# A mixture-of-experts kernel on one core: weight conversions gathered into two of five slots, and tables, gate scalings and transposes at other steps

## The chip, the core and the metric

The kernel runs on one core of a Trainium2 chip. The core has a matrix engine (TensorE, PE in the profile, with its weight loads as PEld), VectorE (DVE), ScalarE (ACT), GpSimd (POOL) and SyncE (SP), which here issues transfers. Each engine works through its own instructions in order; semaphores order them among each other. The metric is the time of one execution in device microseconds, taken as the median of some runs; less is better. Before the change it is 967.4 us (runs from 965.36 to 968.28).

## The reference

Three things in a row: attention over 32 heads with a threshold below the row's maximum, a mixture of 8 experts in which each of 2304 tokens goes to one expert, and a feed-forward block with weights in float64 on the host (`w_in`, `w_out` reach the kernel as pairs of 32-bit words).

```python
def _attn_ref(q, k, v, tau):            # 4 batches, 8 heads, 576 rows, 64 wide
    scores = scale * np.matmul(q, k.transpose(0, 1, 3, 2))
    thresh = np.max(scores, axis=-1, keepdims=True) - tau
    ...
    return np.matmul(attn, v)

def _moe_ref(x, modality_id, w_gate, modality_bias, w1, w2):     # 2304 tokens, 512 wide, 8 experts
    logits = x @ w_gate + modality_bias[modality_id]
    e_idx = np.argmax(logits, axis=1)
    ...
    for e in range(E):
        h = np.maximum(x[mask] @ w1[e], 0.0)                     # 512 -> 1024
        out[mask] = gate_w[mask, None] * (h @ w2[e])             # 1024 -> 512
    return out

def _moe2_ref(x, w_in, w_out):                                   # 512 -> 2048 -> 512
    h = x @ w_in
    g = h * (1.0 / (1.0 + np.exp(-1.702 * h)))
    return g @ w_out
```

## The kernel before

Every product is made of three in a rounded 32-bit format: a matrix is split into an upper half (ScalarE's cast, names that end in h) and a lower half (VectorE's subtraction, names that end in l), and upper x upper, upper x lower and lower x upper are added up in PSUM.

The kernel has three stages on the core's time line. Attention runs until about 316 us. From 316 to some 546 us run five **slots** of one expert each: four with 512 tokens, the last with 264 (`SLOT_ROWS`). From there to the end run the **last blocks**, five blocks of tokens through the feed-forward weights.

The order on every engine is that in which the code issues instructions; no scheduler moves them. The loop over slots s and steps f = 0 to 7 (from line 1364) fixes it. One step does this:

- the first product S1(s, f), 12 matmuls on line 973 with xh, xl (the slot's tokens, transposed) and ah, al (a quarter of the expert's w1 serves two steps); then hh (ScalarE) and hl (VectorE) from its result. The second product S2, 12 matmuls on line 1017 with hh, hl and bh, bl (w2), trails by two steps (`LAG`);
- `split(g, i)` converts a quarter of the weights, ra to ah and al (i = 0) or rb to bh and bl (i = 1): ah, al of quarter g + 1 in even steps, bh, bl of quarter g in odd steps. `load` issues the transfers of ra and rb, 512 KB each, two quarters ahead, on SyncE's queue;
- tokens of the next slot: `gather_slot` on GpSimd's queue at two steps early in the slot (`F0`), four tiles xg of 128 rows; `scale(t)` multiplies a tile by its gate on ScalarE (line 1218), for all tiles at step 2 in slot 0 and at step 3 later; then four items of `xprep`, each four transposes into one PSUM tile (line 945), xh on ScalarE and xl on VectorE, one at each of the steps that `XP0` (slot 0) and `XP` (later) give: steps 3 to 6 in slot 0, 4 to 7 later. In the last slot the same places take `xsplit` for the first last block (lines 960 and 961);
- **conversions** of the feed-forward weights (`conv`, a `Pipe`): each has three parts, one step or more apart: the load of cv_raw (512 KB, SyncE), the upper part (cv_a on ScalarE, then four VectorE operations, lines 1143 to 1146), the lower part (wi_h or wo_h on ScalarE, wi_l or wo_l on VectorE, lines 1151 and 1152). There are 15 in the slots; one begins at every odd step from slot 1 on: four in each of the slots 1 to 3, three in slot 4;
- `att.sides(6)` twice a step: side work in small pieces, in slot 0 and 1 above all the routing tables for the slots after the first two (`Router.assign("B", ...)`): R, OL (line 861 to 868) on VectorE, sums on TensorE (line 874), the lists for the gathers. A `None` in that list ends a turn.

At the end of a slot its result y (512 x 512) is copied out of PSUM at the next slot's step 1, two tiles each on ScalarE and VectorE, and written by four transfers on SyncE's queue, ahead of the third quarter's weights of that slot. The tiles xg, raw weights and cv_raw have 4, 2 and 2 buffers: a transfer waits until its buffer has been read.

Of the kernel before, what the change touches and what calls it, by code (L numbers as in the profile page):

```python
# [13 lines left out]
ACTF = mybir.ActivationFunctionType  # L14
# [6 lines left out]
DM = H * D  # L21
# [13 lines left out]
CA = (0, 1, 2, 2, 2, 2, 2, 2, 2, 2, 2, 2, 2, 2, 2, 2)  # L35
CB = (0, 0, 0, 1, 0, 1, 0, 1, 0, 1, 0, 1, 0, 0, 0, 0)
HO = True
XP = (0, 0, 0, 0, 1, 1, 1, 9)
XP0 = (0, 0, 0, 1, 1, 1, 1, 9)
NBW = 6  # L40
F0 = (0, 1, 0)
NROW = 2
# [485 lines left out]
SLOT_TILES = tuple(-(-r // 128) for r in SLOT_ROWS)  # L528
# [4 lines left out]
class Router:  # L533
# [168 lines left out]
    def assign(self, ph, gate):  # L702
        nc, wk = self.nc, self.wk[ph]
        first = ph == "A"
# [149 lines left out]
        def low(c0, c1):  # L854
            nc.vector.tensor_tensor(
                OL[:, c0:c1], self.iota.unsqueeze(1).broadcast_to([128, c1 - c0, 128]),
                plf[:, 1, c0:c1].unsqueeze(2).broadcast_to([128, c1 - c0, 128]), op=ALU.is_equal,
            )
# [36 lines left out]
        def compact():  # L895
# [15 lines left out]
            yield  # L911
            self.idx["cB"], self.idx["oB"] = icc, ico

        return [
            None, ranks, pages, starts, limits, slots, inside, counted, places, digits, high,
            lambda: (low(0, 5), values(0)), lambda: (low(5, 10), values(1)), lambda: low(10, n), gate,
            *[None] * (1 if first else NBW), lambda: sum_up(0, n), lists,
            *([] if first else [None] * 12 + [gaps, compact, None, bounds]),
        ]
# [118 lines left out]
def moe_kernel(ctx, tc, kq, v, tau, mid, w_gate, mod_bias, w1, w2, w_in, w_out, out):  # L1038
# [171 lines left out]
    def slot(e_idx, g_rows, raw_tile, w_tile, put):  # L1210
# [1 line left out]
        ev = nc.sync.value_load(e_idx, min_val=0, max_val=NE - 1)  # L1212
        W = {}

        def scale(t):

            g = g_rows[t]
            nc.scalar.activation(g[:, 0:DM], g[:, 0:DM], ACTF.Copy, scale=g[:, DM:DM + 1])  # L1218

        def load(g):  # L1220
            ra = raw_tile("ra", "p (k f) -> p k f", dict(k=4))
# [133 lines left out]
    blocks[0]["load"](1)  # L1355
    att.tail(5)
    for t in range(SLOT_TILES[0]):
        blocks[0]["scale"](t)
    for i, f in enumerate(xq):
        f()  # L1360
        att.tail(2)
# [3 lines left out]
    for s in range(NS):  # L1365
        blk = blocks[s]
        for f in range(8):
            ffn.step(blk, f, (lambda: blk["split"](0, 1)) if f == 1 and HO else None, mid3=lambda: att.sides(6))
            f0 = F0[min(s, 2)]
            if s + 1 < NS and f in (f0, f0 + 1):  # L1370
# [6 lines left out]
                gq = gq[2:]  # L1377
                if f == f0 + 1:
                    xq = make_slot(s + 1)
            if s + 1 < NS and f == (3 if s else 2):  # L1380
                for t in range(SLOT_TILES[s + 1]):
                    blocks[s + 1]["scale"](t)
            if s + 1 == NS and f == f0:
                last, xq = make_last(0)
# [14 lines left out]
            if conv is None:  # L1399
                if not att.tail(6):  # L1400
                    open_resident()
                    wi, wo = R["wi"], R["wo"]
                    conv = Pipe(
                        [piece("i", i, wi, i) for i in range(NWI)] + [piece("o", i, wo, i) for i in range(NWO)])
            elif "gB" in router.idx and (f % 2 == 1 or len(conv.live) > 1):
                conv.step(f % 2)
            for _ in range((XP0 if s == 0 else XP)[f]):
                if xq:
                    xq.pop(0)()
            att.sides(6)  # L1410
# [131 lines left out]
```

## Time and profile before

| | us |
|---|---|
| median of three runs | 967.4 |
| lowest, highest | 965.36, 968.28 |
| the profiled execution | 968.82 |
| its span, from the first to the last instruction | 967.1 |
| TensorE busy in the span | 919.8 (95%) |
| VectorE, ScalarE, GpSimd busy | 512.9, 458.0, 225.5 |

Work is reckoned on the profiled execution, which took 1.4 us more than the median. A busy TensorE is not one at its peak, since the ends of its pipelined matmuls are modelled; so its times are read here from start to start of whole groups, and its waits from the idle time ahead of a matmul. The column PEclk gives the share of TensorE's clock that was granted: 1.00 is its 2.4 GHz level and 0.50 its 1.2 GHz level.

### The profile page before, as it was taken

How to read it: one execution, taken by the hardware profiler on the slowest of the kernel's cores; microseconds unless marked ns; L12 is line 12 of the kernel's file. 1: busy time of each engine (PE TensorE's matmuls, PEld its weight loads, DVE VectorE, ACT ScalarE, POOL GpSimd, SP SyncE). 2: the span in 40 equal slices, each digit the busy share in tenths (PEclk: the TensorE clock that was granted, in tenths of full speed). 3: DMA queues.
4: the chain of work that ended last, by engine and by line, in shares of the span. 5: the costliest groups of instructions: out<-in, count | busy, mean ns of one | idle time of the engine just before them, and what ended most of it. 6: DMA issues, size and time to landing. Idle time of an engine off the chain costs nothing.

```text
span 967.1 us, 13933 instructions
## 1 busy us (share of the span) xinstructions
PE 919.8 (95%) x5015; PEld 740.3 (77%) x5015; DVE 512.9 (53%) x1125; ACT 458.0 (47%) x824; POOL 225.5 (23%) x299
## 2 busy tenths in 40 slices
PE   8899999999988989999998899999999999999995
PEld 7677777777765768778877788888888888888894
DVE  6888888888895374666566768721111111111110
ACT  6677777777776333545354545522322222222221
POOL 4846475476313401010520000010001000100100
PEclk9999999999999999999999899999999999999998
DMA  7655865755405416555456244410001000100100
GB/s 216 156 140 152 223 163 129 181 121 140 104 4 156 120 49 188 194 178 173 167 176 222 105 141 150 146 44 1 23 22 45 6 12 6 43 1 1 44 1 24
DMA packets 64522, 100.71 MB, mean 104 GB/s; under 512 B 10596, under 2 KB 35970, under 8 KB 64450
## 3 DMA queue, kind: packets, MB, share of 16 engines
q1 hardware_dynamic: 61138, 89.84, 31.9%
q0 software_dynamic: 3312, 9.94, 3.1%
q8 instruction: 42, 0.69, 0.3%
q14 instruction: 30, 0.25, 0.1%
HBM read 63.97 MB, written 17.11 MB: 84 GB/s over the span
## 4 chain that ended last, share of the span: by engine, by line
PE 69%; DVE 12%; issue 6%; DMA 5%; ACT 4%; POOL 2%; SPq 1%; POOLq 0%; ACTq 0%; DVEq 0%
PE tr L973 24%; PE sc L998 19%; PE sc L239 8%; PE sc L1017 6%; PE av L353 5%; PE tr L307 4%; DVE e L250 3%; DVE E L280 2%; DMA ra<-in_moe_w_dram 2%; PE tr L383 1%; DVE bl L1233 1%; PE av L349 1%; ACT e L256 1%; ACT xg L1218 1%; PE tr L328 1%
## 5 line engine op out<-in xcount | busy, mean ns | idle before, releaser
L1208 DVE TENSOR_TENSOR hl<-sg,hh 128x512 fp32r<-128x512 f32 (+1 forms) x80 | 51.1, 638 | 269.6 <-ACT hh L1206 269.6
L1205 ACT ACTIVATE sg<-tr 128x512 f32<-128x512 f32 (+1 forms) x80 | 44.5, 556 | 236.8 <-PE tr L973 236.6
L250 DVE TENSOR_SCALAR_CACHE_REDUCE e<-sc,taue 128x576 f32<-128x576 f32 x144 | 116.6, 813 | 31.1 <-PE sc L239 26.4
L256 ACT ACTIVATE e<-e,thr 128x576 f32<-128x576 f32 x144 | 111.3, 776 | 27.9 <-DVE e L250 27.3
L973 PE MATMUL tr<-xl,wi_h 128*128 128x512 f32 (+1 forms) x320 | 119.5, 374 | 1.7 <-DVE xl L961 1.7
L973 PE MATMUL tr<-xh,wi_l 128*128 128x512 f32 (+1 forms) x320 | 119.4, 373 | 0.0
L973 PE MATMUL tr<-xh,wi_h 128*128 128x512 f32 (+1 forms) x320 | 119.1, 372 | 0.0
L239 PE MATMUL sc<-kA,qT 128*128 128x288 f32 x320 | 102.3, 337 | 14.2 <-DVE E L280 10.9
L998 PE MATMUL sc<-wo_h,hh 128*128 128x512 f32 x288 | 114.1, 396 | 0.0
L998 PE MATMUL sc<-wo_h,hl 128*128 128x512 f32 x288 | 113.9, 396 | 0.0
L998 PE MATMUL sc<-wo_l,hh 128*128 128x512 f32 x288 | 113.8, 395 | 0.0
L280 DVE SCALAR_TENSOR_TENSOR E<-sc,thr,e 128x576 f32<-128x576 f32 x128 | 103.6, 815 | 8.4 <-ACT e L256 4.6
L309 ACT COPY AT<-tr 128x512 f32<-128x512 f32 x128 | 73.9, 578 | 39.6 <-PE tr L307 38.9
L239 PE MATMUL sc<-kB,qT 128*128 128x288 f32 x320 | 89.4, 295 | 1.1 <-DMA kB<-kB 0.6
L239 PEld LDWEIGHTS sc<-kA,qT 128*128 128x128 f32 x320 | 60.3, 188 | 30.9 <-issue 19.4
L307 PE MATMUL tr<-ident,E 128*128 128x128 f32 x512 | 76.7, 272 | 0.0
L353 PE MATMUL av<-AT,V 128*64 128x288 f32 x512 | 76.7, 419 | 0.0
L973 PEld LDWEIGHTS tr<-xl,wi_h 128*128 128x128 f32 x320 | 60.1, 188 | 14.5 <-DVE xl L961 2.1
L973 PEld LDWEIGHTS tr<-xh,wi_h 128*128 128x128 f32 x320 | 60.1, 188 | 12.4
L973 PEld LDWEIGHTS tr<-xh,wi_l 128*128 128x128 f32 x320 | 60.3, 188 | 11.6
L1017 PE MATMUL sc<-hh,bl 128*128 128x512 f32 (+1 forms) x160 | 61.4, 384 | 4.8 <-DVE bl L1233 4.8
L998 PEld LDWEIGHTS sc<-wo_h,hl 128*128 128x128 f32 x288 | 54.2, 188 | 13.2
(218 smaller groups left out, 1707.1 us busy)
## 6 DMA issues: line engine op xcount, KB each, us to landing
ra<-in_moe_w_dram SPq DMA_DIRECT2D x20, 512.0 KB
rb<-in_moe_w_dram SPq DMA_DIRECT2D x20, 512.0 KB
F<-in_kq_dram SPq DMA_DIRECT2D x15, 640.0 KB
cv_raw<-in_moe_w_in_dram SPq DMA_DIRECT2D x16, 512.0 KB
cv_raw<-in_moe_w_out_dram SPq DMA_DIRECT2D x16, 512.0 KB
V<-in_vp_dram SPq DMA_DIRECT2D x16, 320.0 KB
kA<-kA SPq DMA_DIRECT2D x15, 320.0 KB
kB<-kB SPq DMA_DIRECT2D x15, 320.0 KB
```

What stands on the lines that cost most here:

```text
L239: nc.tensor.matmul(sc[:, hf, 0:288], l, d[kk][:, c0 + hf * 288:c0 + (hf + 1) * 288], start=(i == 0), stop=(i == len(ops) - 1),)
L250: nc.vector.tensor_scalar(e, d["sc", w][:, :, 0:288], self.taue[:, 0:1], 3.0e38, op0=ALU.add, op1=ALU.min, accum_out=thr)
L256: self.nc.scalar.activation(d["e", w], d["e", w], ACTF.Exp, bias=d["thr", w][:, 0:1], scale=-1.0)
L280: nc.vector.scalar_tensor_tensor(out=E.rearrange("p (a c) -> p a c", a=2), in0=d["sc", w][:, :, 0:288], scalar=d["thr", w][:, 0:1], in1=d[ ...
L307: nc.tensor.transpose(tp[:, kc * 128:(kc + 1) * 128], E[:, k0 + kc * 128:k0 + (kc + 1) * 128], self.ident)
L309: copies.append(lambda: nc.scalar.copy(AT[:, h, :, c * 128:(c + 1) * 128], tp.rearrange("p (k c) -> p k c", k=4)))
L353: nc.tensor.matmul(d["av"][h * 64:(h + 1) * 64, 0:288], d["V"][:, h, kc, :], d["AT"][:, h, kc, hf * 288:(hf + 1) * 288], start=False, stop ...
L973: nc.tensor.matmul(hps[:, 0:T], w[:, kd, :], blk[x][:, kd, 0:T], start=(i == 0), stop=(i == 11))
L998: nc.tensor.matmul(y, h[:, cs], w, start=(f == 0 and i == 0), stop=(f == blk["nf"] - 1 and i == 2))
L1017: nc.tensor.matmul(blk["y"][d], w[:, ds], h[:, 0:T], start=(f == 0 and i == 0), stop=(f == last and i == 2))
L1205: nc.scalar.activation(sg, hps, ACTF.Gelu_apprx_sigmoid)
L1208: return [upper, lambda: nc.vector.tensor_sub(hl, sg, hh.bitcast(F32))]
```

## The change

It moves work; no product is added or removed. Of the parts, the four scalings of slot 0's tokens pass from ScalarE to VectorE (`fast`). In the table list of phase B three more empty places (`rest`) stand ahead of and between the tables. Slot 0 scales two tiles at step 2 and two at step 3 (`SC`), slot 1 four at step 3 as before, slots 2 and 3 all at step 2. The transposes stand at steps 4 to 7 in slots 0 and 1, and at 3 to 6 from slot 2 on (`XP`). Conversions begin at steps 3, 5, 7 of slot 1 and at steps 0, 1, 3, 4, 5, 7 of slots 2 and 3, none in slot 4 (`CV`); a begun one goes on at every step.

```diff
-XP = (0, 0, 0, 0, 1, 1, 1, 9)
-XP0 = (0, 0, 0, 1, 1, 1, 1, 9)
+XP = ((0, 0, 0, 0, 1, 1, 1, 9), (0, 0, 0, 0, 1, 1, 1, 9), (0, 0, 0, 1, 1, 1, 9, 0))
+SC = ((0, 0, 2, 2), (0, 0, 0, 4), (0, 0, 4, 0))
+CV = ((), (3, 5, 7), (0, 1, 3, 4, 5, 7), (0, 1, 3, 4, 5, 7), ())
...
+        rest = [] if first else [None]
         return [
-            None, ranks, pages, starts, limits, slots, inside, counted, places, digits, high,
-            lambda: (low(0, 5), values(0)), lambda: (low(5, 10), values(1)), lambda: low(10, n), gate,
+            None, ranks, pages, starts, limits, slots, inside, counted, places, digits, *rest, high,
+            lambda: (low(0, 5), values(0)), *rest, lambda: (low(5, 10), values(1)), *rest, lambda: low(10, n), gate,
...
-        def scale(t):
+        def scale(t, fast=False):
             g = g_rows[t]
-            nc.scalar.activation(g[:, 0:DM], g[:, 0:DM], ACTF.Copy, scale=g[:, DM:DM + 1])
+            if fast:
+                nc.vector.tensor_scalar_mul(g[:, 0:DM], g[:, 0:DM], g[:, DM:DM + 1])
+            else:
+                nc.scalar.activation(g[:, 0:DM], g[:, 0:DM], ACTF.Copy, scale=g[:, DM:DM + 1])
...
-        blocks[0]["scale"](t)
+        blocks[0]["scale"](t, True)
...
-            if s + 1 < NS and f == (3 if s else 2):
-                for t in range(SLOT_TILES[s + 1]):
+            if s + 1 < NS and f < 4:
+                t0 = sum(SC[min(s, 2)][:f])
+                for t in range(t0, min(t0 + SC[min(s, 2)][f], SLOT_TILES[s + 1])):
                     blocks[s + 1]["scale"](t)
...
-            elif "gB" in router.idx and (f % 2 == 1 or len(conv.live) > 1):
-                conv.step(f % 2)
-            for _ in range((XP0 if s == 0 else XP)[f]):
+            elif "gB" in router.idx and (f in CV[s] or conv.live):
+                conv.step(f in CV[s])
+            for _ in range(XP[min(s, 2)][f]):
```

Line numbers of the changed kernel are higher by 1 to 5 (973 becomes 975, 1233 becomes 1238).

VectorE in slot 0, around the hl of step 5 and the tables R and OL; the bl is that of `split(2, 1)`. Before:

```order
L861 TENSOR_TENSOR R<-iota,plf 128x20x48
L855 TENSOR_TENSOR OL<-iota,plf 128x640
L868 TENSOR_TENSOR R<-R,idp 128x20x48
L1197 SCALAR_TENSOR_TENSOR hl<-tr,hh 128x512
L855 TENSOR_TENSOR OL<-iota,plf 128x640
L868 TENSOR_TENSOR R<-R,idp 128x20x48
L855 TENSOR_TENSOR OL<-iota,plf 128x1280
L674 TENSOR_REDUCE g<-L 128x5
L676 TENSOR_SCALAR g<-g 128x5
L678 RECIPROCAL g<-g 128x5
L1233 TENSOR_TENSOR bl<-rb,bh 128x1024
```

After:

```order
L1199 SCALAR_TENSOR_TENSOR hl<-tr,hh 128x512
L862 TENSOR_TENSOR R<-iota,plf 128x20x48
L856 TENSOR_TENSOR OL<-iota,plf 128x640
L869 TENSOR_TENSOR R<-R,idp 128x20x48
L1238 TENSOR_TENSOR bl<-rb,bh 128x1024
L949 SCALAR_TENSOR_TENSOR xl<-av,xh 128x512
L856 TENSOR_TENSOR OL<-iota,plf 128x640
L869 TENSOR_TENSOR R<-R,idp 128x20x48
L1199 SCALAR_TENSOR_TENSOR hl<-tr,hh 128x512
L856 TENSOR_TENSOR OL<-iota,plf 128x1280
```

The hl of step 5 now stands ahead of all tables, and bl after three of them where it stood after six.

VectorE in slot 3, steps 2 and 3: from the hl of step 2 to the bl of `split(1, 1)`. Before:

```order
L1197 SCALAR_TENSOR_TENSOR hl<-tr,hh 128x512
L1233 TENSOR_TENSOR al<-ra,ah 128x1024
L1197 SCALAR_TENSOR_TENSOR hl<-tr,hh 128x512
L1233 TENSOR_TENSOR bl<-rb,bh 128x1024
L1143 TENSOR_SCALAR cv_e<-cv_raw 128x512
```

After:

```order
L1199 SCALAR_TENSOR_TENSOR hl<-tr,hh 128x512
L1238 TENSOR_TENSOR al<-ra,ah 128x1024
L1154 TENSOR_TENSOR wi_l<-cv_a,wi_h 128x512
L1145 TENSOR_SCALAR cv_e<-cv_raw 128x512
L1146 TENSOR_SCALAR cv_a<-cv_a 128x512
L1147 SCALAR_TENSOR_TENSOR cv_a<-cv_a,cv_e 128x512
L1148 SCALAR_TENSOR_TENSOR cv_a<-cv_raw,cv_a 128x512
L1199 SCALAR_TENSOR_TENSOR hl<-tr,hh 128x512
L1238 TENSOR_TENSOR bl<-rb,bh 128x1024
```

A lower part and an upper part of conversions now stand between al and the next hl and bl.

VectorE in slot 4, from the al of `split(3, 0)` in step 4 to the bl of `split(2, 1)` and beyond. Before:

```order
L1233 TENSOR_TENSOR al<-ra,ah 128x1024
L1152 TENSOR_TENSOR wo_l<-cv_a,wo_h 128x512
L1143 TENSOR_SCALAR cv_e<-cv_raw 128x512
L1144 TENSOR_SCALAR cv_a<-cv_a 128x512
L1145 SCALAR_TENSOR_TENSOR cv_a<-cv_a,cv_e 128x512
L1146 SCALAR_TENSOR_TENSOR cv_a<-cv_raw,cv_a 128x512
L961 TENSOR_TENSOR xl<-xg,xh 128x512
L1197 SCALAR_TENSOR_TENSOR hl<-tr,hh 128x264
L1233 TENSOR_TENSOR bl<-rb,bh 128x1024
L1152 TENSOR_TENSOR wo_l<-cv_a,wo_h 128x512
L961 TENSOR_TENSOR xl<-xg,xh 128x512
```

After:

```order
L1238 TENSOR_TENSOR al<-ra,ah 128x1024
L963 TENSOR_TENSOR xl<-xg,xh 128x512
L1199 SCALAR_TENSOR_TENSOR hl<-tr,hh 128x264
L1238 TENSOR_TENSOR bl<-rb,bh 128x1024
L963 TENSOR_TENSOR xl<-xg,xh 128x512
L1199 SCALAR_TENSOR_TENSOR hl<-tr,hh 128x264
L963 TENSOR_TENSOR xl<-xg,xh 128x512
L1199 SCALAR_TENSOR_TENSOR hl<-tr,hh 128x264
```

The conversions are gone from between al and the next hl and bl, and xl (here of the first last block) stands one step earlier.

## Rows read from the trace of the kernel before

**Rows 1.** Stretches: window, length, busy us of PE, PEld, DVE, ACT, POOL, then PEclk.

```profile
463.00:510.00 47.00, 46.10 (x206) 36.91 (x205) 28.58 (x43) 21.57 (x33) 19.42 (x25) 1.00 0.53 176
552.00:955.00 403.00, 403.00 (x1826) 328.83 (x1824) 112.21 (x191) 122.98 (x220) 15.65 (x16) 1.00 0.13 41
```

**Rows 2.** The chain that ended last, in order of time: start, us, what.

```profile
365.95 2.75 PE sc L1017 x12
...
515.95 1.45 PE tr L973 x12
```

**Rows 3.** TensorE's timeline, slot 0: start, us, operation, then idle before and releaser.

```profile
309.56 0.33 PE L945 MATMUL tr<-ident,xg 128*128 128x128 f32 x1 [0.28 <-ACT xg L1218]
...
338.00 0.27 PE L945 MATMUL av<-ident,xg 128*128 128x128 f32 x1
...
343.61 0.40 PE L1017 MATMUL sc<-hh,bh 128*128 128x512 f32 x1
...
358.38 0.51 PE L1017 MATMUL sc<-hh,bl 128*128 128x512 f32 x1 [2.22 <-DVE bl L1233]
```

**Rows 4.** Groups by line (count, busy us, mean ns); ScalarE's timeline in slot 2.

```profile
L1143 DVE TENSOR_SCALAR cv_e<-cv_raw 128x512 uint32<-128x512 uint32 x32 | 13.5, 422 | 3.8 <-DMA cv_raw<-in_moe_w_in_dram 3.3 <-DMA cv_raw<-in_moe_w_out_dram 0.4
L1145 DVE SCALAR_TENSOR_TENSOR cv_a<-cv_a,cv_e 128x512 int32<-128x512 int32 x32 | 22.2, 694 | 1.1
L1232 ACT CAST ah<-ra 128x1024 fp32r<-128x1024 f32 x20 | 20.9, 1043 | 25.1 <-DMA ra<-in_moe_w_dram 25.1
L1233 DVE TENSOR_TENSOR al<-ra,ah 128x1024 fp32r<-128x1024 f32 x20 | 24.5, 1226 | 33.3 <-ACT ah L1232 33.0 <-issue 0.2
...
447.52 0.68 ACT L1142 ACTIVATE cv_a<-cv_raw 128x512 f32<-128x512 f32 x1 [3.06 <-DMA cv_raw<-in_moe_w_in_dram]
```

**Rows 5.** ScalarE's timeline in slot 0, and a stretch of tables there.

```profile
338.24 0.72 ACT L1218 ACTIVATE xg<-xg 128x512 f32<-128x512 f32 x1 [2.97 <-DMA xg<-x_dram,igaA]
...
349.90:357.10 7.20, 6.26 (x30) 4.82 (x28) 7.12 (x10) 2.72 (x4) 0.00 (x0) 1.00 0.00 0
```

**Rows 6.** Short stretches; the number before the last two is the granted clock.

```profile
359.20:362.70 3.50, 3.50 (x10) 2.62 (x9) 0.32 (x1) 0.00 (x0) 0.00 (x0) 0.51 0.36 88
540.10:543.60 3.50, 3.50 (x17) 3.50 (x18) 1.92 (x4) 0.00 (x0) 0.00 (x0) 0.51 0.16 64
338.00:347.00 9.00, 7.34 (x34) 5.16 (x32) 6.83 (x21) 5.36 (x9) 0.00 (x0) 1.00 0.35 120
```

**Rows 7.** The chain's transfers of third weights; a stretch, GB/s last.

```profile
382.53 6.15 DMA ra<-in_moe_w_dram
...
522.35 3.90 DMA ra<-in_moe_w_dram
...
382.00:389.00 7.00, 7.00 (x33) 5.72 (x32) 0.69 (x1) 0.90 (x2) 0.00 (x0) 1.00 0.97 320
```

**Rows 8.** TensorE's timeline, waits from slot 2 to slot 3.

```profile
419.13 0.50 PE L973 MATMUL tr<-xl,ah 128*128 128x512 f32 x1 [0.77 <-DVE over L816]
...
465.83 0.50 PE L973 MATMUL tr<-xl,ah 128*128 128x512 f32 x1 [0.22 <-DVE xl L947]
...
489.74 0.50 PE L1017 MATMUL sc<-hh,bl 128*128 128x512 f32 x1 [0.39 <-DVE bl L1233]
```

**Rows 9.** TensorE's timeline, the last slot.

```profile
510.10 0.37 PE L973 MATMUL tr<-xh,ah 128*128 128x264 f32 x1
...
512.69 0.39 PE L973 MATMUL tr<-xl,ah 128*128 128x264 f32 x1 [1.12 <-DVE xl L947]
...
527.37 0.39 PE L973 MATMUL tr<-xh,ah 128*128 128x264 f32 x1 [1.36 <-ACT ah L1232]
...
539.93 0.40 PE L1017 MATMUL sc<-hh,bl 128*128 128x264 f32 x1 [1.86 <-DVE bl L1233]
...
549.98 0.50 PE L973 MATMUL tr<-xl,wi_h 128*128 128x512 f32 x1 [1.68 <-DVE xl L961]
...
552.00 0.39 PE L973 MATMUL tr<-xh,wi_h 128*128 128x512 f32 x1
```

## The prediction

> **What bounds the kernel now.** I read the busy times by stage first, then the chain of work that ended last in order of time, then TensorE's own idle times in the slots, and for each of them the engine that it waited for. From 552 us on TensorE is busy for 403.00 of 403.00 us at granted clock 1.00 [rows 1]: the last blocks cannot be sped up by anything that this change does, and whatever the slots save comes straight off the end. So the question is what TensorE loses between 316 and 552 us. Its bare price is in the chain: twelve products of 512 columns take 2.75 us, twelve of 264 columns 1.45 us [rows 2]; a step of a full slot is two such groups, 5.5 us, a step of the last slot 2.9 us. What exceeds these is waiting, or half clock. Recorded idle times run some 0.3 to 0.4 us short of the loss from start to start, because the ends of products are modelled; I say which one I use.
>
> **Scaling on VectorE, ahead of slot 0.** TensorE's first group of transposes waits for ScalarE's scaling of xg, in the row 0.28 us and from start to start some 0.8 [rows 3]. The four scalings become VectorE work, behind the last mask in its order, and a tensor-scalar operation of 128x512 takes 0.42 us there [rows 4] against 0.72 on ScalarE [rows 5]. Bounds 0.3 and 1.0; I take **0.8 off**.
>
> **Slot 0, gate scalings.** ScalarE does all four in step 2; the fourth stands at 338.24 after 2.97 us of waiting for its gather [rows 5], and behind it, in order, stand the weights of step 4. From the transposes at 338.00 to the second product at 343.61 [rows 3] TensorE needs 0.36 + 2.75 us and takes 5.61: 2.5 lost, and 0.3 more just behind. Afterwards only two scalings stand ahead of that conversion, and the transposes come a step later. The fourth gather lands when it did, so the second product of step 2 still waits for its lower weights: 338.24 + 0.72 (scaling) + 1.04 (upper half, ah or bh) + 1.23 (lower half, al or bl) [rows 4] = 341.2, with TensorE there at 340.9. Some 0.3 stays; **2.4 off**, bounds 1.5 and 2.8.
>
> **Slot 0, tables.** From 349.9 to 357.1 VectorE is busy for 7.12 of 7.20 us with the list tables [rows 5] and bl stands behind them; the product waits 2.22 us for bl [rows 3], and right after that the granted clock is 0.51 for 3.5 us [rows 6], which costs half of 3.4: 1.7. Together 3.9 (4.0 from start to start). Afterwards only three of the tables (R, OL, R, some 2.9 us) stand ahead of bl, behind a step that has none: hl ends at about 348.5 in the old time, tables at 351.4, bl at 352.6, and TensorE, 2.8 us earlier than before, wants it at 353.1. The margin is half a microsecond, so bounds 2.5 and 4.0; **4.0 off**. The cover is that half microsecond: without it the rest of a bl (up to 1.2) comes back. The column write x_dram<-g on SyncE's queue also passes behind one weight pair, so these weights no longer hold ScalarE up.
>
> **Slot 1.** With three empty places more, the lists are added up one step (5.5 us) later, and the four gathers that follow run beside the writes of y and the load of the third weights instead of ahead of them. That load took 6.15 us here, with gathers close by, and 3.90 in the last slot with none [rows 7]. The loads moved 320 GB/s there [rows 7], and four gathers are 4 x 270 KB = 1.08 MB: 3.4 us if all of it goes ahead. Bounds 0 and 3.4 us. The old landing was already delayed by the same gathers, so I stay near the low end: **1.0 on**. The Trainium skill ("DMA: Bandwidth & Descriptors", Issuing engines are not separate DMA queues) says that transfers issued by any engine run on the same 16 DMA engines and interleave; that the gathers come from GpSimd's queue gives them no lane of their own. By that alone the upper end would hold and the total would be 953.1; the rows above (6.15 beside gathers, 3.90 without) agree in sign and show less than that.
>
> **Between the slots.** Three times TensorE waits at a slot's edge or between transposes for the last xl, which stands behind a conversion on VectorE: 0.77 us at the first (the row names a tiny operation, over, that stands right behind that xl on VectorE), 0.22 at the last [rows 8], 1.9 in all from start to start. Slot 1 loses a conversion ahead of that point, slots 2 and 3 make their transposes a step earlier. **1.9 off**, bounds 1.0 and 1.9.
>
> **Slots 2 and 3, six conversions.** One conversion is 2 x 0.42 + 2 x 0.69 us on VectorE and a subtraction of 0.69 [rows 4], 2.9 us; two more are 5.8. VectorE was busy 28.58 of 47.00 us in slot 3 [rows 1], so it goes to some 34.4, 73%: it fits as a total. What counts is the order. In step 2 a conversion now stands between al and the next bl. Counted from the landing of the third weights: ah and al to 2.3 us, wi_l and the four operations to some 5.5 (their raw weights land last of three transfers), then hl and bl to 7.3; before, with only scalings in between, bl was done after 5.6, as the bl that ended the wait at 489.74 was. Slot 2, whose load lands earlier, has that much room; slot 3 has none, its product already waited 0.39 us [rows 8]. There the gathers and id writes now run a step earlier, away from that load, which gives back 1 to 2 us. Old loss 1.2, new 2.2: **1.0 on**, bounds -1.2 and 6.
>
> **The last slot.** 41.9 us pass from its first product, 510.10, to the second group of the last blocks, 552.00 [rows 9]. Bare: 15 narrow groups at 1.45, two wide ones of slot 3 and one of the last blocks at 2.75, 30.0. So 11.9 are lost. Conversions stand behind three of the waits: xl in step 0 (1.12), bl at 539.93 (1.86), xl L961 at 549.98 (1.68) [rows 9], and the second of them is followed by half clock (540.10, three such stretches in all [rows 6]), 1.7 more. That is 6.4, and 7.6 from start to start. In the changed order these three places hold no conversion but for the first, where xl now stands a step ahead. The rest, 4.3, is another chain: the third weights are issued behind the four writes of y and land at 526.25 (522.35 + 3.90 [rows 7]); the first product that needs them starts at 527.37 after 1.36 us [rows 9], waits again for al, and half clock follows. Without the clock's 1.6 that chain costs 2.7, and it stays. VectorE copies y some 0.5 us earlier relative to TensorE, so 2.2 remain; whether the clock falls again is open, and I take that it doesn't. **9.6 off**, bounds 5.0 and 10.5. The conversions that left are hidden in slots 2 and 3; there they are paid for above.
>
> **Sum.** -0.8 - 2.4 - 4.0 + 1.0 - 1.9 + 1.0 - 9.6 = -16.7 us. The profiled execution took 968.8 us (span 967.1): 952.1. The median of the runs shown is 967.4, 1.4 below it, so the forecast is **950.7 us**.
>
> **Rivals.** *The load stays the limit of the last slot.* If the third weights land no earlier and the third wait merely moves into the fourth weights, the slot gives back 4.6 instead of 9.6: 955.7. For it: 3.90 us of transfer in a step of 2.9. Against it: the fourth weights lose the raw-weight loads that shared the queue with them.
> *The clock falls in the new waits.* In slots 1, 3 and 4 short waits for late weights remain; if each brings 3.4 us at 0.51, three cost 5.1: 955.8. For it: two falls in the last slot of before, each right behind a wait of about 2 us. Against it: 338 to 347 us lost 2.8 us in three waits and was granted 1.00 throughout [rows 6]. The Trainium skill ("TensorE: Matmul & The Clock Gate", HAM oscillation) states that waits which recur tile by tile each bring the low clock again; the rows bear that out for some waits only.
> *Slower than before.* Raw weights late for every conversion. ScalarE, in order, waited 3.06 us for one of them at 447.52 [rows 4]. Six such waits are 18.4 us in a slot; beside 34.4 us of VectorE work that waits behind them, 52.8 for 47: 5.8 a slot, and with the clock falling three times in each, 5.1 more: 21.8 for both, so 950.7 + 21.8 = 972.5. It decides from some 2.6 us of waiting per conversion on, all in series. Against it: one of the four loads in slot 2 was that late, and upper and lower half stand a step apart.
> *Crowding alone*, the upper end of the term for slots 2 and 3 and of slot 1: 950.7 + 5 + 2.4 = 958.1.
> *No move of the total.* The changed order shows the moves as the diff names them, so this needs the losses to eat the gains, between the last two.
>
> **Chances.** Forecast 0.55 (948 to 953.5), the load 0.14, the clock 0.14, crowding 0.10, slower 0.03, and 0.04 for less than 948, where no new wait arises (-16.7 - 1.0 - 2.2 = 947.5). A measurement tells 0.3%, 2.9 us, from no change: faster 0.94, same 0.03, slower 0.03. The range takes the forecast's spread, the load and the clock, and half of crowding: **946.5 to 958.5**.
>
> **What would show it.** In the changed profile: no granted clock of 0.5 near 355 us; the wait for bl in slot 0 gone; slot 1 starting some 7 us earlier; no wait for xl L963 at the end of the last slot and none for bl in its step 6, but still one for ah behind ra in step 4; the second group of the last blocks starting at 535 to 536 us. A wait for bl in step 2 of slot 3 of 1 to 2.5 us is the price I expect; over 5 us, or waits in every step of slots 2 and 3, would make the prediction wrong, as would a last slot of more than 37 us.

## The result, and the profile after

The changed kernel takes **958.8 us**, the median of seven runs from 956.3 to 962.3, against 968.3 us before (seven runs, 965.4 to 971.2): a ratio of 0.991, 95% interval 0.988 to 0.993. It is faster, but by 9.5 us and not by the 16.7 us of the forecast, and just above the range, which ended at 958.5. In a second set, beside the experiments, it took 961.3 us against 968.3: 0.993 (0.992 to 0.994).

The profiled execution took 962.34 us, its span 960.6; it is the slowest of the seven, 3.6 us above their median, so what its stages lose adds up to more than the median's miss. The first section of its page (engine, busy us, share of the span, instructions) reads:

```profile
PE 917.0 (95%) x5015; PEld 738.8 (77%) x5015; DVE 515.2 (54%) x1129; ACT 454.5 (47%) x820; POOL 224.8 (23%) x299
```

TensorE is busy for 917.0 us where it was 919.8, so of the 6.5 us by which the span is shorter 3.7 are time in which it stood idle, and 2.8 are shorter recorded times of the same products. To find the places, I cut the line at the first product of each slot (stretch, length, busy us of PE, PEld, DVE, ACT, POOL, then PEclk, DMA share, GB/s):

```profile
315.71:361.78 46.07, 44.20 (x210) 35.69 (x208) 29.14 (x59) 19.19 (x32) 10.81 (x19) 1.00 0.37 108
361.78:412.50 50.72, 48.06 (x231) 38.06 (x230) 24.19 (x40) 20.42 (x30) 4.04 (x4) 1.00 0.48 155
412.50:459.69 47.19, 46.38 (x211) 37.48 (x210) 37.22 (x66) 25.39 (x39) 8.76 (x9) 1.00 0.63 213
459.69:508.82 49.13, 47.40 (x205) 38.25 (x204) 34.07 (x53) 23.43 (x37) 15.19 (x21) 0.97 0.54 179
508.82:545.81 36.99, 33.02 (x217) 30.91 (x216) 19.02 (x28) 16.52 (x27) 0.00 (x0) 0.91 0.48 171
546.00:949.00 403.00, 402.87 (x1824) 328.64 (x1823) 112.14 (x192) 122.00 (x219) 15.61 (x16) 1.00 0.12 41
```

The last of these rows answers to the second of [rows 1]: the last blocks are as full as before, 402.87 of 403.00 us. Slot by slot, between the same products, against the same cuts in the trace of before and against what the forecast's terms add up to:

| us | before | forecast | after | after, second profile | after with ra first |
|---|---|---|---|---|---|
| start to the first product of slot 0 | 316.7 | 315.9 | 315.7 | 316.6 | 316.0 |
| slot 0 | 51.9 | 45.5 | 46.1 | 47.3 | 45.7 |
| slot 1 | 47.3 | 48.3 | 50.7 | 50.2 | 47.0 |
| slot 2 | 47.2 | 45.8 | 47.2 | 47.9 | 46.0 |
| slot 3 | 47.0 | 47.6 | 49.1 | 46.8 | 46.0 |
| slot 4, to the second group of the last blocks | 41.9 | 32.3 | 37.0 | 35.6 | 31.8 |
| from there to the end of the span | 415.1 | 415.1 | 414.8 | 415.3 | 415.0 |

(The forecast's terms were put where their waits end: the one between the slots lies in slots 2 and 3. The last column is an experiment, below.) So attention's end and slot 0 came out nearly as forecast; slot 1 cost 2.4 us more than reckoned, slots 2 and 3 some 1 to 3 us together, and the last slot gave back 4.9 to 6.3 us instead of 9.6. (The second profile is that of the same kernel in the second set, 961.37 us.)

What TensorE waits for at these places is on its timeline (start, us, operation, tiles, forms; in brackets the idle time before and who ended it):

```profile
308.58 0.33 PE L947 MATMUL tr<-ident,xg 128*128 128x128 f32 x1 [0.31 <-DVE xg L1221]
...
340.94 0.50 PE L1019 MATMUL sc<-hh,bl 128*128 128x512 f32 x1 [0.75 <-DVE bl L1238]
...
358.67 0.39 PE L1019 MATMUL sc<-hh,bh 128*128 128x512 f32 x1
...
386.06 0.50 PE L975 MATMUL tr<-xh,ah 128*128 128x512 f32 x1 [1.09 <-ACT ah L1237]
...
391.21 0.50 PE L1019 MATMUL sc<-hh,bl 128*128 128x512 f32 x1 [0.76 <-DVE bl L1238]
...
439.22 0.50 PE L1019 MATMUL sc<-hh,bl 128*128 128x512 f32 x1 [0.81 <-DVE bl L1238]
...
487.11 0.50 PE L1019 MATMUL sc<-hh,bl 128*128 128x512 f32 x1 [1.73 <-DVE bl L1238]
...
526.82 0.59 PE L975 MATMUL tr<-xh,ah 128*128 128x264 f32 x1 [3.51 <-ACT ah L1237]
...
528.08 0.59 PE L975 MATMUL tr<-xh,al 128*128 128x264 f32 x1 [0.45 <-DVE al L1238]
...
545.81 0.40 PE L975 MATMUL tr<-xh,wi_h 128*128 128x512 f32 x1
```

Read against [rows 3, 8, 9]: the first transposes wait for VectorE's scaling as long as they did for ScalarE's (0.31), but the row stands 0.98 us earlier; 0.69 of that is already there at an attention product ahead of all scaling (301.57 against 302.26 us). The product behind the tables (358.38 before, 2.22 us for bl) now goes through without one: at 358.67 stands the group after it. The waits at the slots' edges (419.13, 465.83, 512.69) and at the end (549.98) have gone. New is a chain in slot 1, ah, then al, then bl, at 386.06 to 391.21, and a wait for bl in step 2 of slot 2, at 439.22; the one in step 2 of slot 3 (0.39 at 489.74) has grown to 1.73, at 487.11. And the wait for ah in the last slot has grown: 3.51 us where it was 1.36.

The granted clock (the number before the last two) answers to [rows 6]:

```profile
350.00:357.00 7.00, 7.00 (x35) 5.77 (x34) 6.97 (x10) 2.71 (x4) 0.00 (x0) 1.00 0.28 78
488.10:491.60 3.50, 3.50 (x12) 2.68 (x11) 1.63 (x2) 0.00 (x0) 0.34 (x1) 0.51 0.86 333
525.60:532.50 6.90, 5.23 (x22) 4.93 (x23) 4.19 (x6) 4.61 (x7) 0.00 (x0) 0.51 0.39 123
```

No half clock in slot 0 any more, but a new stretch in slot 3, right behind the wait for bl, and twice as long a one (6.8 us by the trace's clock record) in and behind the wait for ah in the last slot.

Two rows of the chain that ended last, the transfers of the third weights in slot 1 and in the last slot, answer to [rows 7]:

```profile
375.87 9.08 DMA ra<-in_moe_w_dram
...
520.36 5.34 DMA ra<-in_moe_w_dram
```

They took 9.08 and 5.34 us, where it was 6.15 and 3.90. In the second profile the same two took 9.0 and 4.0 us, read from their issue to the cast on ScalarE that waited for them; so the long transfer of slot 1 recurs, that of the last slot does not. What both have in common is their place: behind the writes of y. In slot 1 the first two rows are GpSimd's first and last gather, the next two SyncE's y writes and the ra behind them, the last one the stretch of all three (its last numbers: clock, DMA share, GB/s):

```profile
373.14 1.04 POOL L1062 DMA_INDIRECT xg<-x_dram,igaB  x1 [14.69 <-PE sc L1019]
...
377.10 1.00 POOL L1062 DMA_INDIRECT xg<-x_dram,igaB  x1 [0.30 <-issue]
...
373.25 2.42 SPq L1273 DMA_DIRECT2D y_first<-y  x4
375.87 0.39 SPq L1227 DMA_DIRECT2D ra<-in_moe_w_dram  x1
...
373.00:385.00 12.00, 11.97 (x53) 9.48 (x51) 2.08 (x3) 1.44 (x4) 4.04 (x4) 1.00 0.90 295
```

Four gathers, four writes and three weight transfers leave within 4.7 us; for 12 us the DMA engines are 90% busy at 295 GB/s.

### The profile page after: what moved, and what is told of

Same layout as the page of the kernel before. It is cut to its first block, busy times and chain, and to the rows that moved or that the text cites. A ratio compares the mean times of both kernels' runs of the same rounds, so it can differ in the third digit from the quotient of the medians.

```text
span 960.6 us, 13951 instructions
## 1 busy us (share of the span) xinstructions
PE 917.0 (95%) x5015; PEld 738.8 (77%) x5015; DVE 515.2 (54%) x1129; ACT 454.5 (47%) x820; POOL 224.8 (23%) x299
## 4 chain that ended last, share of the span: by engine, by line
PE 70%; DVE 10%; issue 8%; DMA 6%; ACT 3%; POOL 1%; SPq 1%; POOLq 0%; ACTq 0%; DVEq 0%
PE tr L975 24%; PE sc L1000 19%; PE sc L240 9%; PE sc L1019 6%; PE av L354 4%; PE tr L308 4%; DVE e L251 3%; DVE E L281 2%; DMA cv_raw<-in_moe_w_in_dram 2%; DMA ra<-in_moe_w_dram 2%; DMA xg<-x_dram,igaA 1%; PE tr L384 1%; DVE bl L1238 1%; PE av L350 1%; ACT e L257 1%
## 5 line engine op out<-in xcount | busy, mean ns | idle before, releaser
L240 PE MATMUL sc<-kA,qT 128*128 128x288 f32 x320 | 102.2, 336 | 14.3 <-DVE E L281 11.1
L975 PE MATMUL tr<-xh,ah 128*128 128x512 f32 (+1 forms) x160 | 61.8, 386 | 5.3 <-ACT ah L1237 4.6
```

Source lines behind the costliest of these rows:

```text
L240: nc.tensor.matmul(sc[:, hf, 0:288], l, d[kk][:, c0 + hf * 288:c0 + (hf + 1) * 288], start=(i == 0), stop=(i == len(ops) - 1),)
L975: nc.tensor.matmul(hps[:, 0:T], w[:, kd, :], blk[x][:, kd, 0:T], start=(i == 0), stop=(i == 11))
```

## The experiments

Two theories stood against each other. **Late weights**: the third quarter's ra, issued behind the four y writes, sets the slots wherever something else is taken away or added beside it. **Conversions**: VectorE and ScalarE, in order, still hold back al and bl, in slots 2 and 3 now instead of slot 4. A third, the **clock**, could explain any 2 to 5 us by stretches of half clock. All times stand beside runs of the kernel before on the same chip (968.3, 968.4, 967.4 and 968.0 us in the four sets).

### The changed kernel once more

> The changed kernel once more, as the measure for the runs beside it. Seven runs of it lie between 956.3 and 962.3 us, at mean granted clocks between 0.995 and 0.990. If half-clock stretches come and go from run to run, spans and mean clocks move together again, about 1.7 us for each stretch of 3.4 us, and the lowest runs are those without any; the profile then shows another number of stretches between 300 and 550 us than the three of the first. If each wait that is long enough brings its stretch every time, the profile shows the same three at the same places (S2 of slot 3 step 2, and two behind the wait for ah in the last slot).

961.3 us (959.9 to 962.0), 0.993. The profile has one half-clock stretch between 300 and 550 us, not three: in the last slot, behind the wait for ah (2.11 us). The wait for bl in slot 3 was 1.19 us and no half clock followed; slot 3 took 46.8 us instead of 49.1. But spans and mean clocks move together only loosely (959.9 us at 0.992, 961.8 at the same), since this profile lost time elsewhere instead: 47.3 us in slot 0, where ScalarE waited 3.83 us for the ra of step 4 (at 337.76 us). In the last slot the third ra was issued 12.0 us after the slot's first product and took 4.0 us, as before the change, and still TensorE waited longer for ah than before (issue, ScalarE's cast, TensorE):

```profile
520.67 0.41 SPq L1227 DMA_DIRECT2D ra<-in_moe_w_dram  x1
...
524.64 1.04 ACT L1237 CAST ah<-ra 128x1024 fp32r<-128x1024 f32 x1 [5.45 <-DMA ra<-in_moe_w_dram]
...
525.74 0.39 PE L975 MATMUL tr<-xh,ah 128*128 128x264 f32 x1 [2.11 <-ACT ah L1237]
```

A stretch of 3.4 us at half clock costs 1.7 us at most: 1.7 in this profile, 5.1 for the three of the first. So the clock is not the 7 to 10 us by which the two sets fall short of the forecast's 16.7.

### ra of the third quarter ahead of the y writes

```diff
+        def load_a(g):
+            ra = W["ra", g] = raw_tile("ra", "p (k f) -> p k f", dict(k=4))
+            nc.sync.dma_start(ra, ...)
         def load(g):
-            ra = raw_tile("ra", "p (k f) -> p k f", dict(k=4))
-            nc.sync.dma_start(ra, ...)
+            if ("ra", g) not in W:
+                load_a(g)
+            ra = W["ra", g]
...
-            ffn.step(blk, f, (lambda: blk["split"](0, 1)) if f == 1 and HO else None, mid3=lambda: att.sides(6))
+            ffn.step(
+                blk, f, (lambda: (blk["split"](0, 1), s and blk["load_a"](2))) if f == 1 and HO else None,
+                mid3=lambda: att.sides(6))
```

> The changed kernel, with the transfer of ra of the third quarter issued in step 1 right behind split(0, 1), ahead of the four writes of y on SyncE's queue, in slots 1 to 4; rb stays behind the writes. Theory of the late load: the wait of 3.5 us for ah in the last slot goes, the slot shrinks from 37.0 to about 31 us, slot 1 from 50.7 to 48 us; the total falls by 5 to 8 us, to 951 to 954. Rival, VectorE and ScalarE behind the conversions hold the last slot: the wait moves to al or bl and the total stays within 1 us of the changed kernel.

**949.8 us** (949.3 to 951.1), 0.982 (0.981 to 0.983): 11.5 us less than the changed kernel beside it, more than was expected. SyncE's timeline in the last slot shows the new order, ra, the four writes, rb:

```profile
504.08 0.39 SPq L1227 DMA_DIRECT2D ra<-in_moe_w_dram  x1
508.59 3.71 SPq L1286 DMA_DIRECT2D y_rest<-y  x4
512.50 0.41 SPq L1235 DMA_DIRECT2D rb<-in_moe_w_dram  x1
```

TensorE's waits from 360 to 545 us (engine and line, who ended the wait: us in total, times, longest) are down to three:

```profile
PE sc L1019 <- DVE bl L1243: 0.9, 2, 0.5
PE tr L975 <- DVE al L1243: 0.4, 1, 0.4
```

and slots 1 and 4, in the form of the table of stretches above, have next to no waits left, at full clock:

```profile
361.65:408.66 47.01, 47.01 (x232) 38.23 (x230) 24.43 (x41) 20.54 (x30) 4.03 (x4) 1.00 0.52 168
500.72:532.51 31.79, 30.88 (x218) 28.66 (x216) 18.76 (x28) 16.51 (x27) 0.00 (x0) 1.00 0.55 199
```

The third ra now leaves 0.5 us after the start of slot 1 and 3.4 us after that of the last slot, where it left 14.1 and 11.5 us after them: there SyncE, in order, had first waited for y to be copied (in the last slot 3.9 us for ScalarE's and 1.4 for VectorE's part), then issued the writes. With it in time all slots are shorter: 3.2 us in slot 1, 1.8 in slot 2, 0.8 in slot 3, 3.8 in slot 4 against the second profile. So the late weights stand behind what the forecast missed; what part the conversions have in it, the next runs ask. With the weights in time, each stage is within 1.6 us of the forecast's, as the table's last column says.

### The gathers of slot 1 earlier

```diff
-NBW = 6
+NBW = 3
```

> The changed kernel with three empty places fewer behind the tables (NBW 3 for 6), so that the lists are added up, and slot 1's gathers issued, one step and a half earlier, as in the kernel before, while the tables stay spread. Theory: the gathers beside the y writes and the third weights cost slot 1 about 3.4 us; slot 1 shrinks from 50.7 to 47 to 47.5 us, slot 0 stays at 46, the total falls by 2.5 to 3.5 us. Rival: slot 1's waits come from VectorE's order (bl, xl) and not from the transfer: slot 1 stays at 50 to 51.

955.7 us (955.0 to 958.6), 0.989: 5.6 us less than the changed kernel beside it, more than expected. The gathers leave 2.2 us after the start of slot 1 (5.8 in the kernel before, 11.4 in the changed one), the third ra takes 3.7 us (issue and ScalarE's cast), and slot 1 has no wait left and takes 45.8 us:

```profile
375.60 0.39 SPq L1227 DMA_DIRECT2D ra<-in_moe_w_dram  x1
...
379.32 1.05 ACT L1237 CAST ah<-ra 128x1024 fp32r<-128x1024 f32 x1 [2.23 <-DMA ra<-in_moe_w_dram]
...
362.46:408.24 45.78, 45.78 (x214) 37.64 (x210) 26.22 (x52) 19.95 (x29) 4.92 (x4) 1.00 0.50 166
```

That is 4.4 to 4.9 us less than in the changed kernel; 0.85 of them is the sum over the lists on TensorE, which stands in slot 0 here. So the gathers' collision costs slot 1 some 3.5 to 4.1 us, the upper bound of 3.4 or a little more, of which the kernel before already paid some 0.6 (47.3 against 45.8 and the 0.85). (The rest of the 5.6 us lies ahead of slot 1, 0.7 us in attention and 1.6 in slot 0, where waits for transfers vary from run to run.)

### The old conversions

```diff
-            elif "gB" in router.idx and (f in CV[s] or conv.live):
-                conv.step(f in CV[s])
+            elif "gB" in router.idx and (f % 2 == 1 or len(conv.live) > 1):
+                conv.step(f % 2)
```

> The changed kernel with conversions begun as in the kernel before (every odd step: 4, 4, 4 and 3 in slots 1 to 4); all else stays changed. If the conversions that left the last slot are worth what the waits there said, the last slot grows from 37.0 to 40 to 42 us, while slots 2 and 3 shrink by 1 to 3.5 us together (no bl wait in step 2 of slot 3): total 1 to 4 us above the changed kernel. Rival, the load of the third weights alone sets the last slot: it stays at 37 and the total falls by 1 to 3 us.

961.4 us (959.3 to 964.4), 0.994: the same as the changed kernel beside it, and not the 1 to 4 us more that were expected. Slots 2 and 3 shrink to 92.7 us together, 2.0 to 3.6 less, the last slot grows to 39.3, 2.3 to 3.7 more:

```profile
412.22:459.57 47.35, 46.15 (x212) 37.65 (x210) 32.42 (x55) 23.55 (x35) 8.33 (x10) 1.00 0.56 190
459.57:504.89 45.32, 45.32 (x206) 37.19 (x204) 28.88 (x43) 21.49 (x33) 17.25 (x20) 1.00 0.52 171
504.89:544.15 39.26, 33.82 (x217) 31.36 (x216) 28.04 (x47) 18.13 (x31) 0.00 (x0) 0.91 0.53 188
```

So with late weights, emptying the last slot of conversions brings nothing on the whole. The last slot did answer, but by less than its waits had promised, and slots 2 and 3 took it back.

### Both together, and each on the kernel before

Conversions and place of ra, one by one and together, on the changed kernel and on the one before: three kernels more, made of the diffs above (for the last of the three, the lines on CV and conv.step in the diff of the change alone).

> The changed kernel with ra first (949.8 us), and its conversions begun at every odd step as in the kernel before. Theory: once the third weights are in time, what stands behind conversions in the last slot shows: the slot grows from 31.8 to 35 to 37 us and the total to 952 to 955. Rival, that the gathering of conversions is worth nothing at all (as with the late load, where undoing it moved nothing): 949 to 950.5, the last slot at 32 to 33.

958.1 us (956.6 to 961.3), 0.990 (0.988 to 0.992), more than expected: with the weights in time the gathering of conversions is worth 8.3 us. The last slot takes 38.4 us against 31.8, 6.8 of it at half clock. In the chain that ended last the conversions stand one by one between al and bl (start, us, engine, tile, line):

```profile
524.25 1.13 DVE al L1243
525.38 0.60 DVE wo_l L1154
525.98 0.34 DVE cv_e L1145
526.32 0.34 DVE cv_a L1146
526.69 0.70 DVE cv_a L1147
...
528.02 0.68 DVE xl L963
...
529.05 1.14 DVE bl L1243
530.24 2.79 PE sc L1019 x11
```

> The kernel before, with ra of the third quarter issued ahead of the writes of y in slots 1 to 4, and nothing else. Theory, that the late load and the conversions stand one behind the other in the last slot: here the load's 4 us there and 1.9 us of small waits in slots 1 and 3 go, the conversions' waits (xl, bl in step 6, xl L961) stay: 3 to 5.5 us less than before, 963 to 965, so less than half of the 11.5 us that the same edit brought on the changed kernel. Rival, that the load cost the same before and after and the edit is simply worth 8 to 11 us by itself: 957 to 960.

964.5 us (963.8 to 966.3), 0.996 (0.995 to 0.998): 3.9 us less than before, a third of what the same edit brings on the changed kernel. What TensorE still waits for in its last slot is behind conversions:

```profile
PE sc L1017 <- DVE bl L1238: 1.9, 1, 1.9
PE tr L973 <- DVE xl L961: 1.7, 1, 1.7
PE sc L1017 <- ACT bh L1237: 1.5, 1, 1.5
PE tr L973 <- DVE xl L947: 1.1, 1, 1.1
```

> The kernel before, with the conversions alone begun as in the changed kernel (3, 6, 6 in slots 1 to 3, none in slot 4). By the forecast's own step the last slot would lose 7.6 us of 41.9 and slots 2 and 3 gain about 1: 961 to 962. Theory of the late load: the xl and bl waits go (4 to 5 us, clock apart) and the wait for ah behind ra in step 4 grows by 1.5 to 3 us: the slot at 38 to 40, the total 965 to 968.

965.0 us (960.5 to 967.8, ten runs), 0.996 (0.994 to 0.998): 3.4 us less than before, where the forecast's own step said 6 to 7. The last slot is down to 36.1 us, lower than expected, but slots 2 and 3 are at 49.9 and 48.2, 3.7 us more than in the kernel before, with waits for bh and bl and half clock at 443.9 us. No wait for an xl is left, and the wait for ah is there, 2.84 us where [rows 9] had 1.36. In slot 0, which this edit does not touch, the wait behind the tables is the same as before (2.21 us, 2.22 in [rows 3]), but full clock followed it, and the slot takes 50.3 us instead of 51.9:

```profile
359.19 0.51 PE L1018 MATMUL sc<-hh,bl 128*128 128x512 f32 x1 [2.21 <-DVE bl L1234]
...
531.25 0.40 PE L974 MATMUL tr<-xh,ah 128*128 128x264 f32 x1 [2.84 <-ACT ah L1233]
```

Together, each against the kernel before of its own set (968.3 or 968.4):

| us | ra behind the y writes | ra ahead of them | difference |
|---|---|---|---|
| changed kernel, conversions as before | 961.4 | 958.1 | -3.2 |
| changed kernel, conversions gathered | 961.3 | 949.8 | -11.5 |
| difference | -0.1 | -8.3 | |

Neither edit is worth much alone; both together give 11.5 us. Two waits stand one behind the other in the last slot, and to remove one shows the other: with ra ahead the gathering gains 6.6 us there, with ra behind 2.3 to 3.7. The rest lies in slots 2 and 3, where the gathered conversions cost 2.0 to 3.6 us with ra behind and nothing with ra ahead (92.1 us against 92.7).

### Both remedies for slot 1

```diff
 (ra ahead of the y writes, as above)
-NBW = 6
+NBW = 3
```

> The changed kernel with ra first and with three empty places fewer behind the tables (gathers of slot 1 ahead of the y writes again). Theory: the gathers cost slot 1 only by way of the third weights, which ra first has brought in time, so nothing is left to gain: 949 to 950.5, slot 1 at 47. Rival, that both edits add up: 945 to 947.

951.2 us (949.1 to 953.5), 0.983: not told apart from ra first alone (0.982). So the gathers had hurt only by way of the third weights, as far as these runs can tell.

### Without the empty places

```diff
-        rest = [] if first else [None]
+        rest = []
```

> The changed kernel without the three empty places between the tables (rest is empty), so that the tables stand in a row in slot 0 and slot 1's gathers go out early, as in the kernel before. By the forecast's terms, corrected by what the gathers cost (3.4 us and not 1.0): slot 0 grows by 3 to 4 us (wait for bl behind the tables, and half clock behind it), slot 1 shrinks by 3 to 4.5 us, and the total stays within 1.5 us of the changed kernel (958.8 to 961.3). Rival, that the split scalings alone give VectorE enough room in slot 0, so that the empty places only harm: slot 0 stays below 47.3 and the total falls to 955 to 957.

957.4 us (955.6 to 958.5), 0.990 (0.988 to 0.992). Slot 0 grows to 48.0 us and slot 1 shrinks to 47.0; the wait behind the tables is back, though no half clock followed it this time:

```profile
355.45 0.50 PE L1019 MATMUL sc<-hh,bl 128*128 128x512 f32 x1 [1.61 <-DVE bl L1238]
```

Its interval overlaps that of the changed kernel (0.991 and 0.993 in its two sets), so it stays open whether the empty places are worth nothing or cost a little; that they bring the 4 us of the forecast on the whole is excluded. The wait that they remove in slot 0 cost 1.9 us here, 4.0 with the half clock in the kernel before; what slot 1 loses to the gathers takes it back.

### No conversion parts in step 2

```diff
-CV = ((), (3, 5, 7), (0, 1, 3, 4, 5, 7), (0, 1, 3, 4, 5, 7), ())
+CV = ((), (3, 5, 7), (2, 3, 4, 5, 6, 7), (2, 3, 4, 5, 6, 7), ())
```

> The changed kernel with the six conversions of slots 2 and 3 begun at steps 2 to 7 instead of 0, 1, 3, 4, 5, 7, so that step 2 has no lower and no upper part between al and the next bl; the third weights stay late. If the conversions in that step cost what the forecast reckoned: the waits for bl in step 2 of slots 2 and 3 (1.1 to 1.6 and 1.5 to 3.4 us) go, total 2 to 4 us below the changed kernel (955 to 958). Rival, that the late third weights alone make these waits: they stay above 0.7 us each, the total within 1.5 us.

956.1 us (953.2 to 957.2), 0.988 (0.985 to 0.990). Both waits for bl are gone, and slots 2 and 3 hold TensorE without a gap, 91.4 us instead of 94.6 to 96.3:

```profile
412.84:458.95 46.11, 46.11 (x211) 37.65 (x210) 35.19 (x61) 25.18 (x38) 8.78 (x9) 1.00 0.66 218
458.95:504.28 45.33, 45.33 (x205) 37.19 (x204) 33.96 (x53) 23.82 (x38) 16.23 (x21) 1.00 0.57 194
```

So those waits need both, late weights and conversions in step 2: either remedy removes all but 0.4 us of them. Both remedies together were not run.

### rb ahead as well, and the transposes later

```diff
-                blk, f, (lambda: (blk["split"](0, 1), s and blk["load_a"](2))) if f == 1 and HO else None,
+                blk, f, (lambda: (blk["split"](0, 1), s and blk["load"](2))) if f == 1 and HO else None,
...
-                if g + 2 < 4:
+                if s and f == 1:
+                    pass
+                elif g + 2 < 4:
                     blk["load"](g + 2)
```

> The changed kernel with both ra and rb of the third quarter ahead of the writes of y. What is left in the kernel with ra first is 0.7 us in step 2 of slot 3 and 0.65 and 0.75 us in steps 4 of the last slot, all for lower weights; with rb earlier the waits for bl go: 948 to 949.5. Rival: the writes of y stand later and ra of the fourth quarter with them, whose al is then late: 950 to 952.

950.5 us (948.3 to 951.8), 0.982 (0.980 to 0.985): no difference from ra alone, and not the 948 to 949.5 that were expected.

```diff
 (ra ahead of the y writes, as above)
-XP = (..., (0, 0, 0, 1, 1, 1, 9, 0))
+XP = (..., (0, 0, 0, 0, 1, 1, 1, 9))
```

> The changed kernel with ra first (949.8 us), and its transposes back at steps 4 to 7 from slot 2 on, as in the kernel before; conversions stay gathered. By the forecast's term the xl of each slot's edge stands behind a conversion in step 7 again: 1.1 to 1.6 us at the edges from slot 2 to 3 and from 3 to 4, and at the end of the last slot only the split of step 7 without a conversion: 1.5 to 3.5 us more in all, 951.3 to 953.3. Rival, the early transposes are worth nothing once the third weights are in time: 949 to 950.5.

951.5 us (951.0 to 954.3), 0.983 (0.982 to 0.985), against 0.982 (0.981 to 0.983) without: not told apart. Nor does the profile bear the term out: there is one wait for an xl, 1.1 us between transposes in slot 2, and none at a slot's edge. What the earlier transposes are worth stays open.

The best kernel of the study is the changed one with ra first, at 949.8 us: 1.8% below the kernel before, and 1.1% below the changed one (0.982 against 0.993 on the same chip).

## Why the forecast was too low

**Right.** That whatever the slots save comes off the end: the last blocks kept their 403 us. The scaling on VectorE (0.8): slot 0 starts at 315.5 to 316.7 us in the eleven profiles built on the changed kernel, 316.0 in the mean, and at 316.4 to 317.5 in the three built on the kernel before, 316.8 in the mean. Counted from the attention product at some 302 us, which stands ahead of the scaling, the eleven take 13.9 us in the mean (13.6 to 14.5) and the three 14.6 (14.4 to 14.9), so some 0.6 belongs to the change and the rest to attention; no run changed the scaling alone. The tables: bl ends at 352.3 us (forecast 352.6 in the old time, 351.8 less the first term), no wait, full clock; the 4.0 came in full in slot 0. But 1.7 of it is half clock that happened to be in the profile from which the term was read: in the kernel before with the new conversions alone the same wait was followed by full clock. That this part came in is luck. Most of the split scalings: with the tables, slot 0 gave back 5.8 of 6.4 us in the first profile and 4.6 in the second. What was left there, 0.75 us before bl at 340.94, is the gather that the forecast put at 0.3. The waits for xl at slot edges went as said, 1.9 us in all, and the conversions' new places are enough for it: with them alone on the kernel before no wait for an xl is left, while with the early transposes and the old conversions one is (1.20 us at 415.98). Of the signs that the prediction named, the half clock near 355 us, the wait for bl in slot 0 and those in step 6 and at the end of the last slot went, and the one for ah stayed; but the second group of the last blocks starts at 545.8 us and not at 535 to 536, and the last slot takes 37.0 us, just at the mark that was to show the prediction wrong.

**Mis-sized: slot 1, "1.0 on".** The bounds were 0 and 3.4 us, and the low end was taken because the old landing "was already delayed by the same gathers". But in the old order the gathers were issued from 374.31 us on, 5.6 us ahead of the first y write, and mostly done when ra came; in the new one they leave together. The transfer took 9.08 us (3.7 with the gathers out of its way), and slot 1 2.9 to 3.5 us more than before. So the choice of the low end was wrong. The rule quoted from the Trainium skill ("DMA: Bandwidth & Descriptors", Issuing engines are not separate DMA queues), that transfers of all engines interleave on the same 16 DMA engines, pointed to the upper end; the trace agrees with it, at 295 GB/s for all three kinds together.

**Wrong: the last slot, "2.2 remain".** The step held that the ra chain there is a constant, 2.7 us, that moves a little earlier. But the xl wait in step 0 that the change removes had been covering it: TensorE came to ah 14.3 us after the slot's start instead of 15.7 (14.8 in the second profile), while ra landed 16.9 us after it instead of 16.2 (16.0 in the second profile). The kernel before with the new conversions alone shows the same: the xl wait gone, that for ah at 2.84 us. In the first profile ra had been issued 0.7 us earlier, as forecast, but took 1.4 us longer; in the second it took no longer than before, so that part is not the rule, and its cause stays open (rb follows on the queue some 0.6 us behind in all three traces). So the wait grew to 3.5 and 2.1 us, and the clock, of which the prediction said "I take that it doesn't" fall, fell for 6.8 and 3.4 us. In all 7.0 and 5.6 us are lost in that slot and not 2.2. (The forecast's 9.6 off is 9.7 by its own terms, 7.6 + 1.6 + 0.5.)

**Mis-sized: slots 2 and 3.** The mechanism was as told, a chain counted from the landing of the third weights through a conversion to bl; the run without conversion parts in step 2 shows it. But slot 2 has no more room than slot 3, 0.8 to 1.3 us of wait; and in slot 3 the wait, within the 1 to 2.5 us expected, was followed by half clock in one profile of two.

**The chances.** Three rivals, *the load stays the limit*, *the clock falls in the new waits*, *crowding alone*, had 0.38 between them, each with its own time, as if they excluded one another. They need the same thing, the third weights behind the y writes, and so came together. By the forecast's own prices the load (5.0) and slot 1 (2.4) alone bring 950.7 to 958.1, the upper edge of the range; slots 2 and 3 with the clock came on top. (The load's rival had the wait move to the fourth weights; it stayed at the third and grew.) With ra first every stage comes out nearly as reckoned, 949.8 us in all. But that is another kernel, so it bears out the other terms as a whole and not the step on the last slot.

## What to carry to other kernels

Before you price a wait that goes, look one step further down the same path: what lands next, and how long before TensorE gets there? A wait that is removed moves everything behind it earlier, except what hangs on a transfer, and the next late transfer takes the gain. A load that something waits for should not stand on its queue behind a write that nobody waits for. And rivals that have one cause are added up, not weighed against each other.

## What the runs showed of the hardware

The half clock is less bound to the length of a wait than the profile of before suggested. Behind a wait of 1.73 us for bl in slot 3 it fell, and behind 1.19 us in another execution of the same kernel it did not; the wait of 2.03 us for ah in the last slot of the kernel without empty places and of 1.61 us in its slot 0 were followed by full clock. Like waits at the same place differ too: behind the tables in slot 0 the clock fell after 2.22 us in the kernel before [rows 6] and did not after 2.21 us in the same kernel with the new conversions. And in the kernel before with ra first it fell at 341.2 us, behind three waits of 0.5 to 0.6 us, which in the kernel before were followed by full clock (338 to 347 us in [rows 6]). What decides it these runs don't tell. With ra first there was no such stretch between 300 and 550 us, and its five runs lie within 1.9 us of each other; the seven of the changed kernel spread over 6.0, but the six of its second set over 2.2 only.
